# The first addition of a three-tap convolution, for batches 4, 5 and 6, by accumulating DMAs from SBUF to SBUF in place of VectorE

## The chip, the cores and the metric

The kernel runs on one core of a Trainium2 chip. The metric is the device time of one execution in microseconds (us), smaller is better; a kernel is run several times and the median is taken. Profiles are of one execution each; times in them count from the start of the profile's span.

## The reference

Two stages run in sequence: a linear attention with a normalisation, and a feed-forward block whose gate comes from a convolution along the sequence. Shapes: 8 batches, 8 heads of 64, sequence 576, model width 512, inner width 1024.

```python
kv  = einsum('bhsd,bhse->bhde', k, v)
o   = einsum('bhsd,bhde->bhse', q, kv)
x   = o / sqrt(mean(o*o, -1) + 1e-6) * g_norm        # heads side by side: (8, 576, 512)
h   = maximum(x @ w_in, 0)                           # (8, 576, 1024)
c   = conv_w[0]*h[s-1] + conv_w[1]*h[s] + conv_w[2]*h[s+1]   # per channel, zero outside the sequence
out = (h * sigmoid(c)) @ w_out                       # (8, 576, 512), float32
```

## The kernel before

Features lie on the 128 partitions and the sequence along the free dimension, in bf16. The inner width of 1024 makes eight feature tiles (index f), the model width four (index t). Two batches share one tile of x and one tile of h.

The order of all work is written out by hand in one string, ORDER. Its tokens are operations with their indices, such as `hm.6.0`; a loop calls them in turn, and a last loop fixes that each engine runs its instructions in exactly this order. Semaphores between the engines come from the tile framework. The operations that matter here, with the engine and the line in the profile of before:

- `Lq`, `Lk`, `Lv` (L148): loads of a batch of q, k, v from HBM, issued from GpSimd's queue, cast to bf16 on the way.
- `sp.b.t` (L411, TensorE) and `mu.b.t` (L417, VectorE): the normalising factor is spread over the partitions in PSUM, and x is made of it, one of four tiles t of batch b.
- `hm.b.f` (L434, TensorE): one feature tile of h from all four tiles of x; `re.b.f` (L440, ScalarE) takes it out of PSUM with a relu.
- the convolution of a chunk c, for a pair j of feature tiles (f = 2j and 2j+1): `ta.c.f` (L459, VectorE) makes the three products of a feature tile with its tap weights, in a buffer `tap` of three parts; there are two such buffers. `ad.c.j` adds the three parts for both tiles of the pair, in two instructions: the first part, shifted by one, is added to the middle one (L466), then the last part, shifted the other way (L467). `sg.c.j` (L473, ScalarE) takes the sigmoid in place, and `mg.c.j` (L479, VectorE) multiplies h by it.
- `om.p.m` (L524, TensorE): 128 rows of the output of batch pair p, from all eight tiles of h; `ea` (L530, ScalarE) copies them from PSUM and `st` (L540) stores them, from SP's queue.

Chunks of the convolution are, by the table CONV: batch 0 (on TensorE), 1, 2 and 3 together, 4 and 5 together (chunk 3), 6 (chunk 4), and 7 (chunk 5). Chunk 3's `tap` has two batches, chunk 4's has one. So an `ad` of chunk 3 adds 2 x 2 x 575 elements on each partition in each instruction, one of chunk 4 2 x 575.

PSUM has two pools: three buffers (`ps_a`) for h, x's factors and the transposes, two (`ps_b`) for the output rows. Since each engine's order is fixed, an instruction that waits holds up all that stand behind it on its engine.

Of the kernel before, what the change touches and what calls it, by code (L numbers as in the profile page):

```python
# [54 lines left out]
AL = mybir.AluOpType  # L55
# [4 lines left out]
BUFS = {'a': 3, 'b': 2, 'q': 2, 'k': 2, 'v': 2, 'qT': 5, 'sq': 8, 'o32': 8, 'xT': 2, 'h': 2, 'tap': 2, 'row': 8, 'w': 2, 'gate': 3}  # L60

ORDER = """
di.4 di.7 di.6 qt.0.0 qc.0.0 qt.0.1 kv.0.0.1 kvc.0.0.1.0 kvc.0.0.1.1 ot.0.0 di.5 kv.0.1.1 sq.0.0 qc.0.1 on.0
di.2 kvc.0.1.1.0 nl.0 kvc.0.1.1.1 ot.0.1 sq.0.1 kv.0.2.1 nx.0 on.1 kvc.0.2.1.1 mu0.0 kvc.0.2.1.0 di.1 Lk.1
Lv.1 nl.1 nx.1 kv.0.3.1 ot.0.2 kvc.0.3.1.1 sq.0.2 on.2 kvc.0.3.1.0 nl.2 mu0.1 ot.0.3 sq.0.3 on.3 ws.1 Lq.1
ws.2 nx.2 mu0.2 nl.3 ws.0 nx.3 mu0.3 hm.0.0 hm.0.7 re.0.7 re.0.0 kv.1.0.4 kvc.1.0.4.0 Lw hm.0.5 Lk.2 Lv.2 Lq.2
re.0.5 hm.0.2 re.0.2 qt.1.0 kvc.1.0.4.1 hm.0.4 re.0.4 qc.1.0 ot.1.0 qt.1.1 qc.1.1 ot.1.1 sq.1.0 oc.1.1 sq.1.1
ot.1.2 sq.1.2 di.0 ot.1.3 sq.1.3 oc.1.3 oc.1.2 ss.1 ln.0 hm.0.1 Lk.3 ex.0 re.0.1 Lv.3 hm.0.6 di.3 Lq.3 oc.1.0
hm.0.3 cv.0.0 re.0.6 sl.0 sp.1.0 mu.1.0 re.0.3 sv.0.0 cv.0.4 sp.1.1 kv.2.0.4 sv.0.4 Lk.4 sp.1.3 mu.1.1
kvc.2.0.4.1 mv.0.0 mu.1.3 sp.1.2 mu.1.2 cv.0.6 cv.0.2 sv.0.6 hm.1.0 mv.0.6 qt.2.1 sv.0.2 mv.0.4 mv.0.2 qc.2.1  # L70
kvc.2.0.4.0 hm.1.1 re.1.0 re.1.1 ot.2.3 ta.1.0 cv.0.7 sq.2.3 sv.0.7 hm.1.4 Lv.4 oc.2.3 cv.0.5 qt.2.0 ta.1.1
ad.1.0 re.1.4 sv.0.5 sg.1.0 hm.1.5 re.1.5 qc.2.0 ot.2.1 mg.1.0 cv.0.1 sq.2.1 sv.0.1 oc.2.1 ot.2.0 sq.2.0
oc.2.0 kv.3.0.4 kvc.3.0.4.0 ta.1.4 Lq.4 qt.3.0 qc.3.0 hm.1.6 hm.1.7 kvc.3.0.4.1 ta.1.5 mv.0.7 re.1.6 re.1.7
ot.3.0 oc.3.0 sq.3.0 mv.0.1 qt.3.1 cv.0.3 qc.3.1 ot.3.3 sv.0.3 oc.3.3 ta.1.6 Lk.5 Lv.5 ta.1.7 ot.3.2 sq.3.3
sq.3.2 ot.3.1 oc.3.2 mv.0.3 ot.2.2 kv.4.0.4 sq.3.1 sq.2.2 oc.3.1 hm.1.2 ss.2 re.1.2 ss.3 ad.1.3 ln.1 ex.1
kvc.4.0.4.0 Lq.5 qt.4.1 qt.4.0 ad.1.2 mv.0.5 qc.4.1 hm.1.3 qc.4.0 kvc.4.0.4.1 om.0.2 re.1.3 oc.2.2 sl.1 sp.2.0
mu.2.0 sg.1.3 sp.3.2 mu.3.2 sp.2.2 om.0.0 mu.2.2 mg.1.3 sp.2.3 ot.4.2 Lk.6 Lv.6 mu.2.3 ea.0.2 sp.2.1 om.0.3
mu.2.1 oc.4.2 ot.4.3 sq.4.2 ea.0.0 ta.1.2 sp.3.3 mu.3.3 sq.4.3 oc.4.3 sp.3.0 mu.3.0 ta.1.3 kv.5.0.4 sg.1.2
sp.3.1 kvc.5.0.4.0 hm.2.0 hm.2.5 ea.0.3 mu.3.1 ad.1.1 re.2.0 re.2.5 hm.2.4 qt.5.0 kvc.5.0.4.1 re.2.4 qc.5.0
sg.1.1 qt.5.1 qc.5.1 hm.2.2 re.2.2 ot.4.1 oc.4.1 sq.4.1 st.0.0 mg.1.2 hm.3.4 re.3.4 Lq.6 Lk.7 Lv.7 Lq.7 mg.1.1  # L80
hm.3.5 re.3.5 ot.5.3 oc.5.3 sq.5.3 hm.3.2 hm.3.3 re.3.2 ot.5.0 hm.2.3 ta.2.4 re.3.3 sq.5.0 ta.2.5 re.2.3
ot.5.2 sq.5.2 oc.5.0 oc.5.2 om.0.4 ot.4.0 ta.2.2 ot.5.1 hm.3.6 oc.4.0 ad.2.2 ta.2.3 sq.5.1 ea.0.4 sq.4.0
om.0.5 ss.4 ss.5 oc.5.1 re.3.6 qt.6.0 ea.0.5 ln.2 qt.7.0 qt.6.1 ex.2 ad.2.1 qc.6.0 om.0.8 ea.0.8 sg.2.1 qc.6.1
om.0.1 sl.2 sp.4.0 ea.0.1 sp.4.2 qc.7.0 sp.5.1 kv.6.0.4 mu.4.0 hm.3.0 mu.5.1 mu.4.2 mg.2.1 sp.5.0 hm.3.1
mu.5.0 re.3.0 re.3.1 sp.4.3 kv.7.0.4 kvc.7.0.4.0 kvc.6.0.4.0 sp.5.3 kvc.7.0.4.1 hm.2.1 re.2.1 mu.4.3 ta.2.0
hm.2.6 sp.4.1 st.0.8 mu.5.3 kvc.6.0.4.1 sg.2.2 sp.5.2 ta.2.1 mu.4.1 om.0.7 hm.3.7 re.2.6 ad.2.0 mg.2.2 re.3.7
sg.2.0 mu.5.2 om.0.6 hm.2.7 re.2.7 hm.4.0 ea.0.6 hm.5.1 ta.2.6 re.5.1 hm.4.3 re.4.3 ta.2.7 ea.0.7 hm.5.0
re.5.0 re.4.0 hm.5.5 re.5.5 hm.5.2 re.5.2 st.0.3 ad.2.3 mg.2.0 st.0.7 qt.7.1 hm.4.1 hm.5.4 sg.2.3 re.4.1
qc.7.1 re.5.4 hm.4.5 re.4.5 hm.4.2 ot.6.1 re.4.2 ta.3.0 oc.6.1 hm.5.3 sq.6.1 mg.2.3 ot.6.3 om.1.5 ot.6.0
re.5.3 ot.7.1 oc.6.3 sq.6.3 ea.1.5 ot.6.2 sq.6.0 oc.7.1 om.1.2 ta.3.1 ta.3.2 oc.6.0 ta.3.3 ad.3.0 ot.7.3  # L90
oc.6.2 sq.6.2 ea.1.2 st.0.6 om.1.6 ot.7.0 sq.7.1 hm.4.4 om.1.8 sg.3.0 re.4.4 ea.1.6 sq.7.0 sq.7.3 ot.7.2
st.1.2 ad.3.1 sq.7.2 ea.1.8 oc.7.3 om.1.3 ea.1.3 ss.6 ss.7 ln.3 hm.5.6 st.0.1 mg.3.0 ta.3.4 re.5.6 ta.3.5
ad.3.2 om.1.4 hm.4.7 st.0.5 ex.3 om.1.0 oc.7.2 sl.3 oc.7.0 st.1.5 sp.6.0 mu.6.0 sp.6.3 re.4.7 mu.6.3 sg.3.1
ea.1.4 hm.4.6 re.4.6 sp.7.0 mu.7.0 hm.5.7 re.5.7 sp.6.2 om.1.7 st.0.4 ea.1.0 mg.3.1 sp.7.3 ea.1.7 mu.6.2
sg.3.2 ta.3.6 sp.6.1 sp.7.2 mu.7.2 om.1.1 mu.6.1 hm.6.0 re.6.0 st.0.2 hm.6.2 re.6.2 ta.3.7 mg.3.2 ad.3.3
ea.1.1 st.1.1 hm.6.1 re.6.1 hm.6.3 re.6.3 hm.6.4 re.6.4 hm.6.5 sg.3.3 mu.7.3 ta.4.2 sp.7.1 hm.6.6 mu.7.1
ta.4.3 mg.3.3 hm.6.7 re.6.5 re.6.7 hm.7.6 hm.7.2 re.7.6 st.1.0 ad.4.1 re.6.6 re.7.2 hm.7.3 sg.4.1 hm.7.4
ta.4.4 hm.7.0 re.7.4 ta.4.5 mg.4.1 re.7.0 hm.7.7 hm.7.5 ad.4.2 st.1.8 ta.4.0 ta.4.1 re.7.7 hm.7.1 om.2.2
sg.4.2 mg.4.2 ea.2.2 st.1.7 om.2.8 ea.2.8 st.2.8 ta.4.6 ad.4.0 sg.4.0 ta.4.7 ad.4.3 om.2.0 re.7.5 ea.2.0
mg.4.0 om.2.7 ta.5.6 om.2.4 sg.4.3 mg.4.3 ta.5.7 ea.2.7 ea.2.4 ta.5.4 om.2.3 re.7.3 st.2.0 ea.2.3 ad.5.3  # L100
sg.5.3 re.7.1 ta.5.5 om.2.1 ea.2.1 ad.5.2 mg.5.3 st.1.6 st.1.4 om.2.6 ta.5.2 sg.5.2 mg.5.2 st.2.1 ea.2.6
st.2.7 ta.5.0 st.2.4 ta.5.3 ta.5.1 om.2.5 ea.2.5 om.3.0 om.3.1 ad.5.1 ad.5.0 ea.3.0 st.3.0 ea.3.1 st.3.1
sg.5.1 om.3.2 mg.5.1 om.3.3 sg.5.0 ea.3.2 ea.3.3 st.1.3 mg.5.0 st.2.5 om.3.8 ea.3.8 st.3.3 st.2.3 st.2.6
om.3.5 ea.3.5 st.3.5 st.2.2 st.3.8 om.3.6 st.3.2 ea.3.6 st.3.6 om.3.4 ea.3.4 st.3.4 om.3.7 ea.3.7 st.3.7
"""


# [1 line left out]
def kernel(  # L109
# [11 lines left out]
    nc = tc.nc  # L121
    B, H, S, D = q.shape
# [33 lines left out]
    def load_w_in(eng, i):  # L156
# [9 lines left out]
        out=ident, in_=ident, compare_op=AL.not_equal, fill=1.0,  # L166
# [71 lines left out]
    T = {}  # L238
# [222 lines left out]
                h_tile(p)[:, f, bs, :].rearrange("p b s -> p (b s)"), cw[:, col:col + 1])  # L461

    @op
    def ad(c, j):
        tap = T["tap", c, j].rearrange("p m f b s -> p m (f b) s")
        nc.vector.tensor_add(tap[:, 1, :, 1:], tap[:, 1, :, 1:], tap[:, 0, :, :S - 1])  # L466
        nc.vector.tensor_add(tap[:, 1, :, :S - 1], tap[:, 1, :, :S - 1], tap[:, 2, :, 1:])  # L467

    @op
# [116 lines left out]
```

## Time and profile before

| | us |
|---|---|
| median of 3 runs | 204.3 (202.88 to 204.7) |
| span of the profiled execution, first to last instruction | 201.4 |
| TensorE busy | 175.6 (87%) |
| VectorE busy | 155.5 (77%) |
| ScalarE busy | 149.9 (74%) |
| GpSimd busy | 25.3 (13%) |
| L466, first additions, 20 instructions | 19.8 |
| L467, second additions, 20 instructions | 20.1 |

The profile comes with no time of its own for the profiled execution beside its span; the median of the runs is 2.9 us above that span. The granted clock of TensorE is full throughout. GpSimd's last load is issued at 81.7 us. The work of chunks 3 and 4 on VectorE lies between 120 and 174 us, that of chunk 5 from 172 to 189 us; the last 40 matmuls of the output follow.

### The profile page before, as it was taken

The page shows a single profiled execution, that of the slowest core. Times are in us where ns is not written, and L with a number is a line of the kernel's source. Part 1 is how long each engine was busy: PE and PEld are TensorE (multiplying, and loading weights), DVE is VectorE, ACT ScalarE, POOL GpSimd, SP SyncE. Part 2 cuts the span into 40 slices and gives each one's busy share as a digit, 9 for nine tenths or more (in the row PEclk, how much of TensorE's full clock was granted, in tenths as well). Part 3 has the DMA queues.
Part 4 walks back from the last instruction along what each step waited for, and adds up shares of the span by engine and source line. Part 5 has one row for each costly group of instructions (what it writes and reads, how often), then busy time and mean ns, then how long its engine had stood idle before and what let it go on. Part 6 is the DMA issues. An engine that isn't in the chain of part 4 may idle for free.

```text
span 201.4 us, 4356 instructions
## 1 busy us (share of the span) xinstructions
PE 175.6 (87%) x1783; PEld 111.7 (55%) x1801; DVE 155.5 (77%) x325; ACT 149.9 (74%) x230; POOL 25.3 (13%) x38
## 2 busy tenths in 40 slices
PE   0057389799998999999999999999999999999792
PEld 0044057477775557766576776445667774444340
DVE  3096931368879799799899999989799999999400
ACT  2008816995999989999778899999978865684532
POOL 7383303103132303100000000000000000000000
PEclk9999999999999999999999999999999999999999
DMA  5999999999999999970200020080005001423654
GB/s 129 143 215 315 201 204 205 204 203 204 203 192 203 201 204 173 200 119 5 104 3 3 0 104 3 0 312 2 3 0 208 0 3 48 161 107 116 248 229 188
DMA packets 26295, 27.03 MB, mean 134 GB/s; under 512 B 1292, under 2 KB 21284, under 8 KB 26276
## 3 DMA queue, kind: packets, MB, share of 16 engines
q0 software_dynamic: 20368, 16.78, 52.1%
q1 hardware_dynamic: 5908, 9.98, 13.1%
q8 instruction: 14, 0.23, 0.5%
q14 instruction: 5, 0.04, 0.1%
HBM read 32.52 MB, written 9.44 MB: 208 GB/s over the span
## 4 chain that ended last, share of the span: by engine, by line
PE 60%; DVE 26%; ACT 6%; DMA 3%; issue 2%; SPq 1%; DVEq 0%; ACTq 0%
PE h_ps L434 25%; PE om_ps L524 18%; DVE tap L459 8%; DVE h L479 4%; PE qt_ps L296 4%; DMA cw_rows<-in_moe_conv_w_dram 3%; DVE tap L467 3%; PE kv_ps L272 3%; PE sp_ps L411 3%; DVE tap L466 3%; PE cv_ps L500 3%; PE o_ps L309 2%; DVE xT L417 2%; ACT tap L473 2%; DVE dg L488 2%
## 5 line engine op out<-in xcount | busy, mean ns | idle before, releaser
L434 PE MATMUL h_ps<-xT,w_in_sb 128*128 128x288 bf16 x512 | 69.9, 291 | 2.9 <-DVE w_in_sb L261 2.2
L524 PE MATMUL om_ps<-w_out_sb,h 128*128 128x512 bf16 x278 | 64.1, 379 | 1.5 <-DVE h L479 1.0
L434 PEld LDWEIGHTS <-w_in_sb 128*128 128x128 bf16 x512 | 49.9, 99 | 18.6 <-DVE w_in_sb L261 2.3
L440 ACT ACTIVATE h<-h_ps 128x576 bf16<-128x576 f32 x64 | 41.0, 656 | 13.5 <-PE h_ps L434 13.2
L524 PEld LDWEIGHTS <-h 128*128 128x128 bf16 x288 | 28.0, 98 | 32.3 <-DVE h L479 1.5
L459 DVE TENSOR_SCALAR tap<-h,cw 128x576 bf16<-128x576 bf16 (+1 forms) x120 | 43.8, 429 | 1.7 <-ACT h L440 1.3
L530 ACT ACTIVATE row<-om_ps 128x512 f32<-128x512 f32 x36 | 22.1, 616 | 15.1 <-PE om_ps L524 14.5
L473 ACT ACTIVATE tap<-tap 128x1152 bf16<-128x1152 bf16 (+1 forms) x20 | 31.1, 1553 | 1.7 <-DVE tap L467 1.5
L417 DVE TENSOR_TENSOR xT<-o,sp_ps 128x576 bf16<-128x576 f32 x28 | 20.1, 749 | 4.0 <-PE sp_ps L411 3.7
L479 DVE TENSOR_TENSOR h<-h,tap 128x1152 bf16<-128x1152 bf16 (+1 forms) x20 | 19.8, 994 | 1.8 <-ACT tap L473 1.8
L467 DVE TENSOR_TENSOR tap<-tap 128x1150 bf16<-128x1150 bf16 (+1 forms) x20 | 20.1, 1004 | 0.7
L303 DVE COPY qT<-qt_ps 128x1152 bf16<-128x1152 bf16 x16 | 11.8, 754 | 11.0 <-PE qt_ps L296 10.9
L466 DVE TENSOR_TENSOR tap<-tap 128x1150 bf16<-128x1150 bf16 (+1 forms) x20 | 19.8, 992 | 0.0
L328 ACT ACTIVATE sq<-o_ps 128x576 bf16<-128x576 f32 x28 | 18.2, 687 | 0.5 <-PE o_ps L309 0.5
L334 ACT ACTIVATE o<-o_ps 128x576 f32<-128x576 f32 x28 | 18.1, 675 | 0.2 <-PE o_ps L309 0.2
L286 ACT ACTIVATE kvbd<-kv_ps 64x256 bf16<-64x256 f32 (+1 forms) x18 | 6.0, 339 | 11.8 <-PE kv_ps L272 11.6
L148 POOL DMA_DIRECT2D k_sb<-in_k_dram x11 | 8.0, 728 | 36.9 <-PE kv_ps L272 36.9
L296 PE MATMUL qt_ps<-ident,q_sb 96*64 96x96 bf16 x384 | 11.2, 217 | 1.2 <-DMA q_sb<-in_q_dram 0.9
L296 PEld LDWEIGHTS <-q_sb 96*64 96x64 bf16 x384 | 9.7, 117 | 3.1 <-issue 2.1
L411 PE MATMUL sp_ps<-wparts,spread 128*128 128x288 bf16 x56 | 9.8, 286 | 0.2 <-DVE xT L417 0.2
L308 PE MATMUL o_ps<-qT,kvbd 128*128 128x64 bf16 x32 | 6.3, 196 | 4.0 <-DVE kvbd L284 1.7
L272 PEld LDWEIGHTS <-k_sb 96*64 96x64 bf16 x384 | 7.9, 122 | 3.3 <-issue 3.3
(57 smaller groups left out, 122.5 us busy)
## 6 DMA issues: line engine op xcount, KB each, us to landing
out_dram<-row SPq DMA_DIRECT2D x36, 256.0 KB, 2.3
q_sb<-in_q_dram POOLq DMA_DIRECT2D x8, 576.0 KB, 11.4
k_sb<-in_k_dram POOLq DMA_DIRECT2D x7, 576.0 KB, 10.6
v_sb<-in_v_dram POOLq DMA_DIRECT2D x7, 576.0 KB, 12.5
w_stage<-in_moe_w_in_dram POOLq DMA_DIRECT2D x1, 1024.0 KB, 9.6
w_out_sb<-in_moe_w_out_dram POOLq DMA_DIRECT2D x1, 1024.0 KB, 20.0
k_sb<-in_k_dram POOLq DMA_DIRECT2D x4, 144.0 KB, 9.1
v_sb<-in_v_dram POOLq DMA_DIRECT2D x4, 144.0 KB, 9.0
```

Of the source, the lines that this page charges most:

```text
L296: nc.tensor.transpose(ps[i * D:(i + 1) * D, tt, r * PS:(r + 1) * PS], q_sb[:, 2 * (2 * u + tt) + i, r * D:(r + 1) * D], ident[:PS, :PS])
L328: nc.scalar.activation(s.rearrange("p (n r) -> p n r", r=R), natural(src), AX.Square)
L417: nc.vector.tensor_mul(x_tile(b)[:, t, :].rearrange("p (e n) -> p e n", e=2), T["o32", b, t].rearrange("p (e n) -> p e n", e=2), T["sp", b ...
L434: nc.tensor.matmul(ps[:, e, :HS], w_in_sb[:, t, f * P:(f + 1) * P], x[:, t, e * HS:(e + 1) * HS], start=(t == 0), stop=(t == NT - 1))
L440: nc.scalar.activation(h_tile(b // 2)[:, f, b % 2, :].rearrange("p (e n) -> p e n", e=2), T["hm", b, f][:, :, :HS], AX.Relu)
L459: nc.vector.tensor_scalar_mul(tap[:, m, f % 2, :, :].rearrange("p b s -> p (b s)"), h_tile(p)[:, f, bs, :].rearrange("p b s -> p (b s)"), ...
L466: nc.vector.tensor_add(tap[:, 1, :, 1:], tap[:, 1, :, 1:], tap[:, 0, :, :S - 1])
L467: nc.vector.tensor_add(tap[:, 1, :, :S - 1], tap[:, 1, :, :S - 1], tap[:, 2, :, 1:])
L473: nc.scalar.activation(tap, tap, AX.Sigmoid)
L479: nc.vector.tensor_mul(h, h, T["tap", c, j][:, 1])
L524: nc.tensor.matmul(ps, h[:, f, m * P:(m + 1) * P], w_out_sb[:, f, :], start=(f == 0), stop=(f == NF - 1))
L530: nc.scalar.activation(T["os", p, m], T["om", p, m], AX.Copy)
```

## The change

For chunks 3 and 4 the first addition leaves VectorE. A new operation `aa.c.j` issues two DMAs from GpSimd's queue, one for each feature tile of the pair; each reads the first part of `tap` and adds it to the middle part in SBUF. The second addition stays on VectorE, as the only instruction of these chunks' `ad`. In ORDER each `aa.c.j` stands right behind the second `ta` of its pair, and two of the `ad` stand later than before:

- `ad.3.2` stood behind `ta.3.5`; it now stands behind `mu.6.3`.
- `ad.3.0` still follows `ta.3.3`, `ad.3.3` still follows `mg.3.2`, `ad.4.1` follows `mg.3.3`, `ad.4.2` follows `mg.4.1`.
- `ad.3.1` still follows `ad.3.0`, `ad.4.0` still follows `ta.4.6`.
- `ad.4.3` stood behind `ta.4.7`; it now stands behind `mg.4.0`.

On VectorE two positions thus differ (`ad.3.2` and `ad.4.3`), beside the eight instructions that are gone; the orders of TensorE, ScalarE and SP are the same.

```diff
     @op
+    def aa(c, j):
+        for f in range(2):
+            tap = T["tap", c, j][:, :, f]
+            nc.gpsimd.dma_start(out=tap[:, 1, :, 1:], in_=tap[:, 0, :, :S - 1], accum_op=AL.add)
+
+    @op
     def ad(c, j):
         tap = T["tap", c, j].rearrange("p m f b s -> p m (f b) s")
-        nc.vector.tensor_add(tap[:, 1, :, 1:], tap[:, 1, :, 1:], tap[:, 0, :, :S - 1])
+        if c not in (3, 4):
+            nc.vector.tensor_add(tap[:, 1, :, 1:], tap[:, 1, :, 1:], tap[:, 0, :, :S - 1])
         nc.vector.tensor_add(tap[:, 1, :, :S - 1], tap[:, 1, :, :S - 1], tap[:, 2, :, 1:])
```

The part of ORDER that changes, before and after, cut to VectorE's and GpSimd's tokens:

```
before: ... ta.3.1 ta.3.2 ta.3.3 ad.3.0 ad.3.1 mg.3.0 ta.3.4 ta.3.5 ad.3.2 sl.3 mu.6.0 mu.6.3 mu.7.0 mg.3.1
        mu.6.2 ta.3.6 mu.7.2 mu.6.1 ta.3.7 mg.3.2 ad.3.3 mu.7.3 ta.4.2 mu.7.1 ta.4.3 mg.3.3 ad.4.1 ta.4.4 ta.4.5
        mg.4.1 ad.4.2 ta.4.0 ta.4.1 mg.4.2 ta.4.6 ad.4.0 ta.4.7 ad.4.3 mg.4.0 ta.5.6 mg.4.3 ...
after:  ... ta.3.1 aa.3.0 ta.3.2 ta.3.3 aa.3.1 ad.3.0 ad.3.1 mg.3.0 ta.3.4 ta.3.5 aa.3.2 sl.3 mu.6.0 mu.6.3 ad.3.2 mu.7.0 mg.3.1
        mu.6.2 ta.3.6 mu.7.2 mu.6.1 ta.3.7 aa.3.3 mg.3.2 ad.3.3 mu.7.3 ta.4.2 mu.7.1 ta.4.3 aa.4.1 mg.3.3 ad.4.1 ta.4.4 ta.4.5
        aa.4.2 mg.4.1 ad.4.2 ta.4.0 ta.4.1 aa.4.0 mg.4.2 ta.4.6 ad.4.0 ta.4.7 aa.4.3 mg.4.0 ad.4.3 ta.5.6 mg.4.3 ...
```

More of the change, by code (lines that the diff above doesn't have):

```diff
@@ L62 @@
 ORDER = """
[L63 to L102, printed above, removed]
@@ L103 @@
-sg.5.1 om.3.2 mg.5.1 om.3.3 sg.5.0 ea.3.2 ea.3.3 st.1.3 mg.5.0 st.2.5 om.3.8 ea.3.8 st.3.3 st.2.3 st.2.6
-om.3.5 ea.3.5 st.3.5 st.2.2 st.3.8 om.3.6 st.3.2 ea.3.6 st.3.6 om.3.4 ea.3.4 st.3.4 om.3.7 ea.3.7 st.3.7
+di.4 di.7 di.6 qt.0.0 qc.0.0 qt.0.1 kv.0.0.1 kvc.0.0.1.0 kvc.0.0.1.1 ot.0.0 di.5 kv.0.1.1 sq.0.0 qc.0.1 on.0 di.2
+kvc.0.1.1.0 nl.0 kvc.0.1.1.1 ot.0.1 sq.0.1 kv.0.2.1 nx.0 on.1 kvc.0.2.1.1 mu0.0 kvc.0.2.1.0 di.1 Lk.1 Lv.1 nl.1 nx.1
+kv.0.3.1 ot.0.2 kvc.0.3.1.1 sq.0.2 on.2 kvc.0.3.1.0 nl.2 mu0.1 ot.0.3 sq.0.3 on.3 ws.1 Lq.1 ws.2 nx.2 mu0.2 nl.3 ws.0
@@ new lines @@
+nx.3 mu0.3 hm.0.0 hm.0.7 re.0.7 re.0.0 kv.1.0.4 kvc.1.0.4.0 Lw hm.0.5 Lk.2 Lv.2 Lq.2 re.0.5 hm.0.2 re.0.2 qt.1.0
+kvc.1.0.4.1 hm.0.4 re.0.4 qc.1.0 ot.1.0 qt.1.1 qc.1.1 ot.1.1 sq.1.0 oc.1.1 sq.1.1 ot.1.2 sq.1.2 di.0 ot.1.3 sq.1.3
+oc.1.3 oc.1.2 ss.1 ln.0 hm.0.1 Lk.3 ex.0 re.0.1 Lv.3 hm.0.6 di.3 Lq.3 oc.1.0 hm.0.3 cv.0.0 re.0.6 sl.0 sp.1.0 mu.1.0
+re.0.3 sv.0.0 cv.0.4 sp.1.1 kv.2.0.4 sv.0.4 Lk.4 sp.1.3 mu.1.1 kvc.2.0.4.1 mv.0.0 mu.1.3 sp.1.2 mu.1.2 cv.0.6 cv.0.2
+sv.0.6 hm.1.0 mv.0.6 qt.2.1 sv.0.2 mv.0.4 mv.0.2 qc.2.1 kvc.2.0.4.0 hm.1.1 re.1.0 re.1.1 ot.2.3 ta.1.0 cv.0.7 sq.2.3
@@ new lines @@
+sv.0.7 hm.1.4 Lv.4 oc.2.3 cv.0.5 qt.2.0 ta.1.1 ad.1.0 re.1.4 sv.0.5 sg.1.0 hm.1.5 re.1.5 qc.2.0 ot.2.1 mg.1.0 cv.0.1
+sq.2.1 sv.0.1 oc.2.1 ot.2.0 sq.2.0 oc.2.0 kv.3.0.4 kvc.3.0.4.0 ta.1.4 Lq.4 qt.3.0 qc.3.0 hm.1.6 hm.1.7 kvc.3.0.4.1
+ta.1.5 mv.0.7 re.1.6 re.1.7 ot.3.0 oc.3.0 sq.3.0 mv.0.1 qt.3.1 cv.0.3 qc.3.1 ot.3.3 sv.0.3 oc.3.3 ta.1.6 Lk.5 Lv.5
+ta.1.7 ot.3.2 sq.3.3 sq.3.2 ot.3.1 oc.3.2 mv.0.3 ot.2.2 kv.4.0.4 sq.3.1 sq.2.2 oc.3.1 hm.1.2 ss.2 re.1.2 ss.3 ad.1.3
+ln.1 ex.1 kvc.4.0.4.0 Lq.5 qt.4.1 qt.4.0 ad.1.2 mv.0.5 qc.4.1 hm.1.3 qc.4.0 kvc.4.0.4.1 om.0.2 re.1.3 oc.2.2 sl.1
@@ new lines @@
+sp.2.0 mu.2.0 sg.1.3 sp.3.2 mu.3.2 sp.2.2 om.0.0 mu.2.2 mg.1.3 sp.2.3 ot.4.2 Lk.6 Lv.6 mu.2.3 ea.0.2 sp.2.1 om.0.3
+mu.2.1 oc.4.2 ot.4.3 sq.4.2 ea.0.0 ta.1.2 sp.3.3 mu.3.3 sq.4.3 oc.4.3 sp.3.0 mu.3.0 ta.1.3 kv.5.0.4 sg.1.2 sp.3.1
+kvc.5.0.4.0 hm.2.0 hm.2.5 ea.0.3 mu.3.1 ad.1.1 re.2.0 re.2.5 hm.2.4 qt.5.0 kvc.5.0.4.1 re.2.4 qc.5.0 sg.1.1 qt.5.1
+qc.5.1 hm.2.2 re.2.2 ot.4.1 oc.4.1 sq.4.1 st.0.0 mg.1.2 hm.3.4 re.3.4 Lq.6 Lk.7 Lv.7 Lq.7 mg.1.1 hm.3.5 re.3.5 ot.5.3
+oc.5.3 sq.5.3 hm.3.2 hm.3.3 re.3.2 ot.5.0 hm.2.3 ta.2.4 re.3.3 sq.5.0 ta.2.5 re.2.3 ot.5.2 sq.5.2 oc.5.0 oc.5.2 om.0.4
@@ new lines @@
+ot.4.0 ta.2.2 ot.5.1 hm.3.6 oc.4.0 ad.2.2 ta.2.3 sq.5.1 ea.0.4 sq.4.0 om.0.5 ss.4 ss.5 oc.5.1 re.3.6 qt.6.0 ea.0.5
+ln.2 qt.7.0 qt.6.1 ex.2 ad.2.1 qc.6.0 om.0.8 ea.0.8 sg.2.1 qc.6.1 om.0.1 sl.2 sp.4.0 ea.0.1 sp.4.2 qc.7.0 sp.5.1
+kv.6.0.4 mu.4.0 hm.3.0 mu.5.1 mu.4.2 mg.2.1 sp.5.0 hm.3.1 mu.5.0 re.3.0 re.3.1 sp.4.3 kv.7.0.4 kvc.7.0.4.0 kvc.6.0.4.0
+sp.5.3 kvc.7.0.4.1 hm.2.1 re.2.1 mu.4.3 ta.2.0 hm.2.6 sp.4.1 st.0.8 mu.5.3 kvc.6.0.4.1 sg.2.2 sp.5.2 ta.2.1 mu.4.1
+om.0.7 hm.3.7 re.2.6 ad.2.0 mg.2.2 re.3.7 sg.2.0 mu.5.2 om.0.6 hm.2.7 re.2.7 hm.4.0 ea.0.6 hm.5.1 ta.2.6 re.5.1 hm.4.3
@@ new lines @@
+re.4.3 ta.2.7 ea.0.7 hm.5.0 re.5.0 re.4.0 hm.5.5 re.5.5 hm.5.2 re.5.2 st.0.3 ad.2.3 mg.2.0 st.0.7 qt.7.1 hm.4.1 hm.5.4
+sg.2.3 re.4.1 qc.7.1 re.5.4 hm.4.5 re.4.5 hm.4.2 ot.6.1 re.4.2 ta.3.0 oc.6.1 hm.5.3 sq.6.1 mg.2.3 ot.6.3 om.1.5 ot.6.0
+re.5.3 ot.7.1 oc.6.3 sq.6.3 ea.1.5 ot.6.2 sq.6.0 oc.7.1 om.1.2 ta.3.1 aa.3.0 ta.3.2 oc.6.0 ta.3.3 aa.3.1 ad.3.0 ot.7.3
+oc.6.2 sq.6.2 ea.1.2 st.0.6 om.1.6 ot.7.0 sq.7.1 hm.4.4 om.1.8 sg.3.0 re.4.4 ea.1.6 sq.7.0 sq.7.3 ot.7.2 st.1.2 ad.3.1
+sq.7.2 ea.1.8 oc.7.3 om.1.3 ea.1.3 ss.6 ss.7 ln.3 hm.5.6 st.0.1 mg.3.0 ta.3.4 re.5.6 ta.3.5 aa.3.2 om.1.4 hm.4.7
@@ new lines @@
+st.0.5 ex.3 om.1.0 oc.7.2 sl.3 oc.7.0 st.1.5 sp.6.0 mu.6.0 sp.6.3 re.4.7 mu.6.3 ad.3.2 sg.3.1 ea.1.4 hm.4.6 re.4.6
+sp.7.0 mu.7.0 hm.5.7 re.5.7 sp.6.2 om.1.7 st.0.4 ea.1.0 mg.3.1 sp.7.3 ea.1.7 mu.6.2 sg.3.2 ta.3.6 sp.6.1 sp.7.2 mu.7.2
+om.1.1 mu.6.1 hm.6.0 re.6.0 st.0.2 hm.6.2 re.6.2 ta.3.7 aa.3.3 mg.3.2 ad.3.3 ea.1.1 st.1.1 hm.6.1 re.6.1 hm.6.3 re.6.3
+hm.6.4 re.6.4 hm.6.5 sg.3.3 mu.7.3 ta.4.2 sp.7.1 hm.6.6 mu.7.1 ta.4.3 aa.4.1 mg.3.3 hm.6.7 re.6.5 re.6.7 hm.7.6 hm.7.2
+re.7.6 st.1.0 ad.4.1 re.6.6 re.7.2 hm.7.3 sg.4.1 hm.7.4 ta.4.4 hm.7.0 re.7.4 ta.4.5 aa.4.2 mg.4.1 re.7.0 hm.7.7 hm.7.5
@@ new lines @@
+ad.4.2 st.1.8 ta.4.0 ta.4.1 aa.4.0 re.7.7 hm.7.1 om.2.2 sg.4.2 mg.4.2 ea.2.2 st.1.7 om.2.8 ea.2.8 st.2.8 ta.4.6 ad.4.0
+sg.4.0 ta.4.7 aa.4.3 om.2.0 re.7.5 ea.2.0 mg.4.0 ad.4.3 om.2.7 ta.5.6 om.2.4 sg.4.3 mg.4.3 ta.5.7 ea.2.7 ea.2.4 ta.5.4
+om.2.3 re.7.3 st.2.0 ea.2.3 ad.5.3 sg.5.3 re.7.1 ta.5.5 om.2.1 ea.2.1 ad.5.2 mg.5.3 st.1.6 st.1.4 om.2.6 ta.5.2 sg.5.2
+mg.5.2 st.2.1 ea.2.6 st.2.7 ta.5.0 st.2.4 ta.5.3 ta.5.1 om.2.5 ea.2.5 om.3.0 om.3.1 ad.5.1 ad.5.0 ea.3.0 st.3.0 ea.3.1
+st.3.1 sg.5.1 om.3.2 mg.5.1 om.3.3 sg.5.0 ea.3.2 ea.3.3 st.1.3 mg.5.0 st.2.5 om.3.8 ea.3.8 st.3.3 st.2.3 st.2.6 om.3.5
@@ L105 @@
+ea.3.5 st.3.5 st.2.2 st.3.8 om.3.6 st.3.2 ea.3.6 st.3.6 om.3.4 ea.3.4 st.3.4 om.3.7 ea.3.7 st.3.7
 """
```

## The prediction

> **What bounds the kernel now.** I read the page first (span, busy shares), then the timelines of TensorE and of VectorE from 120 us on, because all that the change touches runs there, and last the rows that can price a DMA. Between this execution's span, 201.4 us, and the median of the runs, 204.3 us, lie 2.9 us that the trace doesn't show; I add my sum to the span and then these 2.9 us.
>
> ```profile
> span 201.4 us, 4356 instructions
> ...
> PE 175.6 (87%) x1783; PEld 111.7 (55%) x1801; DVE 155.5 (77%) x325; ACT 149.9 (74%) x230; POOL 25.3 (13%) x38
> ```
>
> The second view is TensorE's timeline (start, busy us, line).
>
> ```profile
> 149.29 6.04 PE L434 MATMUL h_ps<-xT,w_in_sb 128*128 128x288 bf16 x48
> ...
> 155.42 10.24 PE L434 MATMUL h_ps<-xT,w_in_sb 128*128 128x288 bf16 x80
> 165.71 22.39 PE L524 MATMUL om_ps<-w_out_sb,h 128*128 128x512 bf16 x101
> 189.09 8.81 PE L524 MATMUL om_ps<-w_out_sb,h 128*128 128x512 bf16 x40 [0.98 <-DVE h L479]
> ```
>
> TensorE runs without a gap from 136 to 188 us and idles 0.98 us before the last 40 matmuls, for VectorE's last product (mg.5.0, done 189.03). With one gap of 0.22 us at 135.8 that is all the idle time that this view marks after 120 us (1.6 us by its busy time, slivers included). So relieving VectorE can bring 0.98 us here at most: TensorE then has no wait on it left. But the reverse doesn't hold, as the third view, VectorE's timeline, shows.
>
> ```profile
> 149.16 1.37 DVE L459 TENSOR_SCALAR tap<-h,cw 128x1152 bf16<-128x1152 bf16 x3
> 150.45 1.35 DVE L479 TENSOR_TENSOR h<-h,tap 128x2304 bf16<-128x2304 bf16 x1
> 151.72 1.35 DVE L466 TENSOR_TENSOR tap<-tap 128x2300 bf16<-128x2300 bf16 x1
> 153.10 1.36 DVE L467 TENSOR_TENSOR tap<-tap 128x2300 bf16<-128x2300 bf16 x1
> 154.38 0.74 DVE L417 TENSOR_TENSOR xT<-o,sp_ps 128x576 bf16<-128x576 f32 x1
> 155.04 0.93 DVE L459 TENSOR_SCALAR tap<-h,cw 128x576 bf16<-128x576 bf16 x3
> 155.88 0.75 DVE L417 TENSOR_TENSOR xT<-o,sp_ps 128x576 bf16<-128x576 f32 x1
> 156.54 0.93 DVE L459 TENSOR_SCALAR tap<-h,cw 128x576 bf16<-128x576 bf16 x3
> 157.38 1.35 DVE L479 TENSOR_TENSOR h<-h,tap 128x2304 bf16<-128x2304 bf16 x1
> 158.65 0.76 DVE L466 TENSOR_TENSOR tap<-tap 128x1150 bf16<-128x1150 bf16 x1
> 159.44 0.76 DVE L467 TENSOR_TENSOR tap<-tap 128x1150 bf16<-128x1150 bf16 x1
> ...
> 188.27 0.76 DVE L479 TENSOR_TENSOR h<-h,tap 128x1152 bf16<-128x1152 bf16 x1 [0.63 <-ACT tap L473]
> ```
>
> These are, in order: ta.3.7, mg.3.2, the two additions of ad.3.3, mu.7.3, ta.4.2, mu.7.1, ta.4.3, mg.3.3, the two additions of ad.4.1. VectorE is also full, and some of its results have no slack: mu.7.1 ends at 156.63 and the first matmuls of batch 7 come some 0.8 us later. VectorE's order is in one line, so a wait inside it delays everything behind it.
>
> **The change part by part.** Removed: 8 first additions (L466), 4 of 128x2300 (1.35 us, a step of 1.38 to the next start) and 4 of 128x1150 (0.75, step 0.79): 8.7 us of VectorE's time. Three of the large ones lie before 139.5 us, where VectorE next waits for ScalarE's Exp (L391, ends 139.5) and then for sp_ps until 142.38; what is saved there goes into these waits.
>
> Added: 16 DMAs on GpSimd's queue, two for each aa; two of 128x2x575 elements (294 KB each) for chunk 3, of 128x575 (147 KB) for chunk 4. That queue is empty after its last load at 81.7 us, so nothing is behind them; SP's stores are untouched and share the DMA engines, which are 13% busy from 157 to 174 us and 37% from 174 to 189. The price is a wait: each ad of chunks 3 and 4 now waits for the landing of a DMA that can be issued only after the second ta of its pair. Call the time from the end of that ta to the landing L2 (chunk 3) and L1 (chunk 4).
>
> No row shows an accumulating transfer, or one from SBUF to SBUF. The nearest:
>
> ```profile
> q1 hardware_dynamic: 5908, 9.98, 13.1%
> ...
> out_dram<-row SPq DMA_DIRECT2D x36, 256.0 KB, 2.3
> ```
>
> ```profile
> 2.51 0.64 POOL L148 DMA_DIRECT2D k_sb<-in_k_dram  x1
> ```
>
> ```profile
> DMA to landing us min/median/max: 5.7/9.9/23.1
> ```
>
> A store from SBUF (128 rows, 8 for each engine) lands in 2.3 us. Its queue's 5908 packets took 13.1% of 16 x 201.4 us, 71 ns each, so 8 rows are 0.57 us and 1.73 us is fixed. GpSimd's issue of a load of 192 rows took 0.64 us. An accumulation must read two operands, so I double the rows: L1 = 0.64 + 1.73 + 2 x 0.57 = 3.5 us; with 16 rows for each engine L2 = 0.64 + 1.73 + 4 x 0.57 = 4.65 us. The lower bound is the fastest store, 2.0 us, for all; the upper the fastest of GpSimd's loads, 5.7 us for 768 rows, for all. I take the middle values since the store is the nearest row: SBUF side, one row for each partition.
>
> Now VectorE's line with these waits. ad.3.0 and ad.3.1 wait (landing 123.9 + 4.65 and 126.7 + 4.65 = 131.3), but mg.3.0 and ta.3.4, ta.3.5 still end near 137, ahead of the Exp at 139.5: cost nothing up to L2 = 7.6 us. The changed order puts ad.3.2 behind mu.6.3, past the idle time that covered it; its landing (137 + 4.65) is over by then, but its second addition, 1.3 us, now stands between mu.6.3 and mu.7.0, so mu.7.0, mg.3.1, mu.6.2 and mu.6.1 are 1.3 us late, and TensorE's hm.6.0, which follows mu.6.1 by 0.05 us, with them. ta.3.7 then ends at 151.75 instead of 150.45; the landing is at 156.4, with only mg.3.2 (1.27) in between; ad.3.3 ends at 157.7, and mu.7.3, ta.4.2, mu.7.1 behind it at 159.8 instead of 156.54: 3.3 us late (L2 - 1.35). Behind the same wait on ScalarE stand sg.3.3 and re.6.5, and on TensorE all of batch 7.
>
> Chunk 4, from the end of mu.7.1 to the end of mg.4.3, took 156.54 to 173.59 = 17.05 us. Now each pair of ta is followed by a landing that has only one or two short instructions to cover it (mg.3.3 1.27; mg.4.1 0.67; mg.4.2 and ta.4.6 1.63; a wait for the sigmoid and mg.4.0, 1.16): all inside L1. So: ta.4.3 0.84, L1, ad 0.76, two ta 1.67, L1, ad 0.76, two ta 1.67, L1, ad 0.76, ta.4.7 0.84, L1, ad 0.76, ta.5.6 0.93, the sigmoid's rest 0.32, mg.4.3 0.75: 10.06 + 4 L1 = 24.06, 7.0 us more. What follows, chunk 5 (173.59 to 189.03), is unchanged and still a line without slack, and the last 40 matmuls follow it. TensorE, 3.3 us late from batch 7 on, would have its 13 chunks of L524 (1.73 us each, from 169.0) done by 191.5, 8 us before mg.5.0 at 199.3. ScalarE's copies out of om_ps stand behind sigmoids that wait for the same landings, and can take most of these 8 us; VectorE still sets the end.
>
> Sum: L2 + 4 L1 - 8.34 = 4.65 + 14.0 - 8.34 = +10.3 us; span 211.7, time 214.6 us. With the bounds 2.0 and 5.7 for both it is +1.7 and +20.2 us: 206.0 and 224.5.
>
> Two rules of the Trainium skill bear on this. The page "DMA: Bandwidth & Descriptors", section "Anatomy of one DMA — SWDGE (gpsimd) path", fits a DMA of GpSimd's to 2.0 us plus its bytes at 436 GB/s; by that L1 = 2.34 and L2 = 2.68, and the time would be 208.0 us, an estimate; no run here shows it for an accumulation. The page "SBUF — State Buffer", section "Who interferes with whom", says that VectorE's two-port instructions, tensor_scalar among them, lock GpSimd out while it writes descriptors. It speaks against the change, since each first DMA of a pair is issued just as the next ta starts. The trace shows a milder thing: where a load's issue (0.77 us) falls on three tensor_scalars, they take 1.21 us instead of 0.92.
>
> ```profile
> 77.15 1.21 DVE L459 TENSOR_SCALAR tap<-h,cw 128x576 bf16<-128x576 bf16 x3
> ```
>
> **The rivals.** *Not slower: the landing is hidden.* If L2 + 4 L1 stay under 8.34 us, 1.67 us each, no stall outlasts what is saved; TensorE's 0.98 us wait goes and nothing else can: 203.3 us, no measurable change. For it: the DMA engines are nearly free then. Against it: not one of the 36 stores landed under 2.0 us, and GpSimd's issue comes on top.
>
> *The accumulation runs at the pace of the loads,* or slower: 5.7 us for each landing, 224.5 us. For it: the loads are GpSimd's only transfers here. Against it: they read HBM with full engines and have three to six times the rows.
>
> *GpSimd and VectorE hold each other up.* On the late line two first DMAs (aa.4.2, aa.4.0) fall on the next ta, 0.29 us each, and five last DMAs may take 0.12 longer to issue (the longest load issue was 0.89): +1.2 us, 215.8 us. Against it: VectorE mostly stands idle or multiplies tensors when the deciding DMA is issued.
>
> That the change doesn't do what it says I exclude: the built order shows the 8 additions gone and the 16 DMAs in place, TensorE's, ScalarE's and SP's orders being the same.
>
> **How the numbers follow.** Forecast 0.68, loads' pace 0.15, mutual hindrance 0.11, hidden 0.06. A measurement here can tell about 1%, 2.0 us, from no change. Faster by that needs more than all of TensorE's idle time after 120 us (1.6 us): 0.01. Within it: 0.05, the hidden landing. Slower: 0.94. The range goes from 207.5 (landings of 2.3 us each) to 224.0, just short of the loads' pace; a bit under 2 in 10 lies outside.
>
> **What would show it.** L466's count falls from 20 to 12, 16 DMA issues appear on GpSimd; their landing, median 2.5 to 4.5 us, decides most. VectorE's idle time before L467's successor (line 471), released by DMAs, should be some 12 to 13 us on the late line (3.4 before the last addition of chunk 3; 2.2, 2.8, 1.9 and 2.3 in chunk 4) and a few hidden us before 137; TensorE should wait 3 us or more in h_ps of batch 7, and the rest of the loss among and before the last om_ps. Wrong I am if that line shows no idle time, if the landing is under 1.7 us or over 6, or if the end is set by something other than VectorE's line.

## The result, and the profile after

The changed kernel takes 210.7 us (median of 4 runs, 210.2 to 211.4), the kernel before 203.6 us (202.5 to 204.7). The ratio is 1.035, 95% interval 1.031 to 1.039: 7.1 us slower.

From the page of the changed kernel: the span, the busy shares, and the groups of the added and the halved work. The columns of a group are busy time, mean ns of one, idle time of the engine before it and what ended most of that; the last two lines are DMA issues with their size and the time to landing.

```profile
span 209.6 us, 4398 instructions
...
PE 178.2 (85%) x1783; PEld 112.3 (54%) x1801; DVE 148.2 (71%) x317; ACT 149.6 (71%) x230; POOL 41.9 (20%) x54
...
L464 POOL DMA_DIRECT2D tap<-tap x16 | 16.7, 1079 | 77.5 <-DVE tap L456 64.5
L471 DVE TENSOR_TENSOR tap<-tap 128x1150 bf16<-128x1150 bf16 (+1 forms) x20 | 20.1, 1004 | 13.8 <-DMA tap<-tap 13.4
...
L470 DVE TENSOR_TENSOR tap<-tap 128x1150 bf16<-128x1150 bf16 (+1 forms) x12 | 11.4, 950 | 0.0
...
tap<-tap POOLq DMA_DIRECT2D x8, 287.5 KB, 4.6
tap<-tap POOLq DMA_DIRECT2D x8, 143.8 KB, 2.8
```

VectorE lost its 8 additions (its busy time falls by 7.3 us), and got 13.4 us of waiting in front of the second additions (L471), ended by the DMAs. Its timeline over the place that the prediction worked through:

```profile
150.49 1.37 DVE L456 TENSOR_SCALAR tap<-h,cw 128x1152 bf16<-128x1152 bf16 x3
151.77 1.35 DVE L483 TENSOR_TENSOR h<-h,tap 128x2304 bf16<-128x2304 bf16 x1
155.64 1.36 DVE L471 TENSOR_TENSOR tap<-tap 128x2300 bf16<-128x2300 bf16 x1 [2.52 <-DMA tap<-tap]
156.92 0.74 DVE L414 TENSOR_TENSOR xT<-o,sp_ps 128x576 bf16<-128x576 f32 x1
...
160.00 1.35 DVE L483 TENSOR_TENSOR h<-h,tap 128x2304 bf16<-128x2304 bf16 x1
162.90 0.77 DVE L471 TENSOR_TENSOR tap<-tap 128x1150 bf16<-128x1150 bf16 x1 [1.55 <-DMA tap<-tap]
163.57 1.76 DVE L456 TENSOR_SCALAR tap<-h,cw 128x576 bf16<-128x576 bf16 x6
165.25 0.75 DVE L483 TENSOR_TENSOR h<-h,tap 128x1152 bf16<-128x1152 bf16 x1
168.51 0.76 DVE L471 TENSOR_TENSOR tap<-tap 128x1150 bf16<-128x1150 bf16 x1 [2.51 <-DMA tap<-tap]
...
174.13 0.76 DVE L471 TENSOR_TENSOR tap<-tap 128x1150 bf16<-128x1150 bf16 x1 [1.56 <-DMA tap<-tap]
...
178.88 0.76 DVE L471 TENSOR_TENSOR tap<-tap 128x1150 bf16<-128x1150 bf16 x1 [1.94 <-DMA tap<-tap]
...
196.40 0.76 DVE L483 TENSOR_TENSOR h<-h,tap 128x1152 bf16<-128x1152 bf16 x1 [0.29 <-ACT tap L477]
```

There is one wait in chunk 3 (ad.3.3) and four in chunk 4 (ad.4.1, 4.2, 4.0, 4.3), each with only one or two short instructions between the end of a ta and the landing. L2, from the start of mg.3.2 (the end of ta.3.7) to ad.3.3, is 155.64 - 151.77 = 3.87 us; L1 is 2.90, 3.26, 3.27 and 3.23 us, in sum 12.66. The last product, mg.5.0, starts at 196.40 instead of 188.27: 8.1 us late, and the span is 8.2 us longer. Of this, 0.3 us is a difference between the two executions from before the first DMA (118.38 instead of 118.09 us for the same multiplication).

### The profile page after: what moved, and what is told of

Same layout as the page of the kernel before. It is cut to its first block, busy times and chain, and to the rows that moved or that the text cites. A ratio compares the mean times of both kernels' runs of the same rounds, so it can differ in the third digit from the quotient of the medians.

```text
span 209.6 us, 4398 instructions
## 1 busy us (share of the span) xinstructions
PE 178.2 (85%) x1783; PEld 112.3 (54%) x1801; DVE 148.2 (71%) x317; ACT 149.6 (71%) x230; POOL 41.9 (20%) x54
## 5 line engine op out<-in xcount | busy, mean ns | idle before, releaser
L528 PE MATMUL om_ps<-w_out_sb,h 128*128 128x512 bf16 x278 | 66.1, 386 | 4.7 <-ACT row L534 4.0
L456 DVE TENSOR_SCALAR tap<-h,cw 128x576 bf16<-128x576 bf16 (+1 forms) x120 | 44.1, 430 | 1.6 <-ACT h L437 1.3
L464 POOL DMA_DIRECT2D tap<-tap x16 | 16.7, 1079 | 77.5 <-DVE tap L456 64.5
L471 DVE TENSOR_TENSOR tap<-tap 128x1150 bf16<-128x1150 bf16 (+1 forms) x20 | 20.1, 1004 | 13.8 <-DMA tap<-tap 13.4
L408 PE MATMUL sp_ps<-wparts,spread 128*128 128x288 bf16 x56 | 9.8, 286 | 2.1 <-DVE xT L414 1.5
L470 DVE TENSOR_TENSOR tap<-tap 128x1150 bf16<-128x1150 bf16 (+1 forms) x12 | 11.4, 950 | 0.0
## 6 DMA issues: line engine op xcount, KB each, us to landing
k_sb<-in_k_dram POOLq DMA_DIRECT2D x7, 576.0 KB, 10.1
```

The source lines that it names most:

```text
L456: nc.vector.tensor_scalar_mul(tap[:, m, f % 2, :, :].rearrange("p b s -> p (b s)"), h_tile(p)[:, f, bs, :].rearrange("p b s -> p (b s)"), ...
L528: nc.tensor.matmul(ps, h[:, f, m * P:(m + 1) * P], w_out_sb[:, f, :], start=(f == 0), stop=(f == NF - 1))
```

## The experiments

**Theory A**, the prediction's: the loss is VectorE's line, waiting for landings that nothing covers, plus what the moved ad add between the mu. **Rival B**: GpSimd's descriptor writing and the transfers slow VectorE itself. **Rival C**: the moved ad are what costs. **Rival D**, for what could be won at best: VectorE, not TensorE, is the bound.

### The parts one by one

`order_only`: the changed order, all additions on VectorE.

```diff
     def aa(c, j):
+        return
         for f in range(2):
...
-        if c not in (3, 4):
+        if True:
```

> The changed order, but no DMA: all additions of chunks 3 and 4 are on VectorE, where the changed order has their ad. Theory A (the loss is VectorE waiting for landings, plus the 1.3 us of ad.3.2 moved between the mu): ad.3.2 now stands there with both additions, 2.66 us, so mu.7.1 is 2.7 us late and the sigmoid's wait of mg.4.0 adds 0.4: some 3 us over before, about 206.7 us, and no idle time before the additions. Rival C (the moved ad are what costs): most of the 7.1 us measured for the whole change is here too, 209 to 211 us. Rival B (GpSimd's descriptor writing and the transfers slow VectorE down): nothing but the order's small price, 204 to 205.

Measured: 208.0 us against 203.9, ratio 1.021 (1.015 to 1.026): +4.1 us.

`only3`: DMAs for chunk 3 alone (`aa` returns for c == 4; `if c != 3` before the first addition).

> Chunk 3's first additions by DMA, chunk 4's back on VectorE, the changed order. A: one landing in the open, ad.3.3: 3.85 us from the end of ta.3.7 to the addition in the changed profile, so 3.85 - 1.35 = 2.5, and 0.5 for mg.4.0's wait: +3.0 us, about 206.6 us. B (cost by number and bytes of the DMAs; chunk 3 has two thirds of the bytes): +4.7 us, 208.3. C: as order_only.

Measured: 207.5 us, ratio 1.016 (1.011 to 1.021): +3.6 us.

`only4`: DMAs for chunk 4 alone, edited likewise.

> Chunk 4's first additions by DMA, chunk 3's back on VectorE, the changed order. A: the four landings of chunk 4, 3.17 us each in the changed profile, cost 4 x 3.17 - 7.05 = 5.6, and ad.3.2 stands with both additions between the mu, 2.66: +8.3 us, about 211.9 us, slower than the whole change although half the DMAs are gone. B (a third of the bytes): +2.4 us and the order's price, 206 to 207. C: as order_only.

Measured: 211.6 us, ratio 1.037 (1.033 to 1.041): +7.7 us.

A's three figures were +3.0, +3.0 and +8.3. Rival B falls as the cause of the loss: chunk 3 has two thirds of the bytes and half of the DMAs, and is no slower with them than without (207.5 against 208.0), while chunk 4's small ones cost 3.6 us over the order alone. C holds for a part, more than A gave it: the order alone costs 4.1 us, 1.0 more than A's sum. The reason is in two lines of `order_only`'s VectorE timeline, of mu.7.1 and of mg.4.0:

```profile
158.52 0.75 DVE L414 TENSOR_TENSOR xT<-o,sp_ps 128x576 bf16<-128x576 f32 x1
...
173.47 0.76 DVE L484 TENSOR_TENSOR h<-h,tap 128x1152 bf16<-128x1152 bf16 x1 [1.23 <-ACT tap L478]
```

mu.7.1 starts 2.64 us late (155.88 before), as the two additions of ad.3.2 between the mu say (2.66). But mg.4.0 then waits 1.23 us for its sigmoid and not 0.4: on ScalarE that sigmoid, at 172.29 us, stands behind a copy of output rows for which ScalarE waits 1.13 us, until TensorE has made the rows (171.79). The tile's additions had ended at 171.40. In chunk 3 the landing in the open and the additions saved are worth the same: mu.7.1 starts at 158.42 in the changed kernel.

### What could be won at best

`left_out`: the order of before, the 8 first additions done by nobody (`if c not in (3, 4)` before L466).

> The order of before, with the 8 first additions of chunks 3 and 4 left out altogether: neither VectorE nor a DMA does them, so the convolution of batches 4 to 6 misses its first tap. This is what the change could bring at best. A (TensorE is the bound, with one wait of 0.98 us on VectorE): -1.0 us, about 202.6 us, although 8.7 us of VectorE's work are gone; TensorE runs without a gap to the end. Rival D (VectorE's line is the bound): -4.5 us, the five steps after 143 us, or more.

Measured: 204.1 us against 203.9, ratio 1.002 (0.998 to 1.005): no difference. Rival D falls, and A's -1.0 us with it. TensorE's timeline shows the wait still there, and the waits show why (engine, line, what it waited for; us in total, times, longest):

```profile
190.71 8.81 PE L525 MATMUL om_ps<-w_out_sb,h 128*128 128x512 bf16 x40 [0.96 <-DVE h L480]
```

```profile
DVE h L480 <- ACT tap L474: 7.3, 6, 3.4
```

The time that VectorE saved became waits for sigmoids, 7.3 us from 100 us on (3.4 of them before mg.3.0, 3.2 in chunk 4). The sigmoids stand on ScalarE in a fixed order, in chunk 4 among copies out of om_ps: the one that mg.4.0 waits for starts at 171.28 us, behind a copy for which ScalarE waits 1.13 us on TensorE, although its additions had ended at 169.50. So VectorE can't run ahead of TensorE here, and arrives at chunk 5, which is unchanged, no earlier than before: behind mg.4.3 it goes on at 175.22 instead of 173.59 us, in an execution whose TensorE is 1.65 us behind that of before already at batch 7 (157.07 and 155.42).

### What a landing is made of

`plain`: the same DMAs without `accum_op`, overwriting the middle part.

> The changed kernel with plain copies of the same bytes in place of the accumulating DMAs, so that the middle part is overwritten and not added to: it prices the accumulation itself. Theory A1 (the time from the end of a ta to the landing is GpSimd's issue and a fixed latency; reading a second operand costs nothing that counts): issue 0.86 and 1.2 us, landing 2.8 us after the issue starts for 147 KB as with the accumulation, about 210.7 us. Theory A2 (an accumulation reads twice and takes twice the engines' time, as the prediction doubled it): 0.57 us less for each landing of chunk 4 and 1.1 less for that of chunk 3: about 207.3 us.

`plain_sp`: the same copies by `nc.sync.dma_start`.

> The same plain copies, issued from SP's queue, among the stores of the output rows; again overwritten, not added to. Theory A3 (GpSimd's issue, 0.86 to 1.2 us, and the second issue waiting for the first, 0.3 us, are a third of each landing): a store's issue is 0.43 us, so each landing comes 0.4 to 0.8 us earlier than in the run with GpSimd's plain copies, 2 to 4 us of time. If the latency lies behind the issue: the same time as with GpSimd's plain copies, or worse by stores held up behind copies that wait.

Measured: 207.1 us, ratio 1.015 (1.008 to 1.022), and 206.4 us, ratio 1.012 (1.005 to 1.019). The pages of the two, first GpSimd's copies, then SP's:

```profile
L464 POOL DMA_DIRECT2D tap<-tap x16 | 11.4, 711 | 78.3 <-ACT h L437 39.1
...
tap<-tap POOLq DMA_DIRECT2D x8, 287.5 KB, 2.6
tap<-tap POOLq DMA_DIRECT2D x8, 143.8 KB, 2.0
```

```profile
tap<-tap SPq DMA_DIRECT2D x8, 287.5 KB, 2.6
tap<-tap SPq DMA_DIRECT2D x8, 143.8 KB, 2.0
```

A1 falls, and the size is near A2's: counted from the start of the issue, 147 KB land in 2.0 us as a copy and 2.8 as an accumulation. (That the second operand takes the time is not shown by this.) Part of the 0.8 us is GpSimd's issue, from these timelines of GpSimd, first the changed kernel's for tiles 4.1 and 4.2, then `plain`'s for 4.1:

```profile
158.77 0.90 POOL L464 DMA_DIRECT2D tap<-tap  x1 [5.85 <-DVE tap L456]
160.10 0.86 POOL L464 DMA_DIRECT2D tap<-tap  x1 [0.43 <-DVE tap L456]
164.75 1.74 POOL L464 DMA_DIRECT2D tap<-tap  x2 [3.79 <-DVE tap L456]
```

```profile
160.08 0.55 POOL L464 DMA_DIRECT2D tap<-tap  x1 [0.67 <-DVE tap L456]
```

The accumulation takes 0.86 us to issue, the copy 0.55; so 0.3 of the 0.8 us is issue and 0.5 lies behind it. The x2 shows why L1 is 2.90 for tile 4.1 and 3.26 for 4.2: two ta of 0.84 us each follow each other, the first issue takes 0.87, and the second DMA starts late. Tile 4.3's L1 of 3.23 us comes of a start some 0.4 us after its last ta (176.04), which the x2 doesn't explain. A3 falls: SP's copies land no sooner than GpSimd's, and the two times, of two runs each, can't be told apart with these intervals. Neither time is a clean price of the landings, since the order alone already takes 208.0 us.

### The landings covered

`cover4`: the order of before; accumulating DMAs for tiles 4.2, 4.0 and 4.3 alone, each second addition moved behind other work. `cover4_vec`: the same order and buffers, all additions on VectorE.

```diff
             if c == 4:
+                two = work.tile([P, 2, 3, 2, n, S], BF16, name="tap", tag="tap", bufs=BUFS["tap"])
+                for s, jj in enumerate((1, 2) if j in (1, 2) else (0, 3)):
+                    T["tap", c, jj] = two[:, s]
...
-        nc.vector.tensor_add(tap[:, 1, :, 1:], tap[:, 1, :, 1:], tap[:, 0, :, :S - 1])
+        if (c, j) not in ((4, 2), (4, 0), (4, 3)):
+            nc.vector.tensor_add(tap[:, 1, :, 1:], tap[:, 1, :, 1:], tap[:, 0, :, :S - 1])
```

```
VectorE, GpSimd: ... ta.4.4 ta.4.5 aa.4.2 mg.4.1 ta.4.0 ta.4.1 aa.4.0 ta.4.6 ad.4.2 ta.4.7 aa.4.3 mg.4.2 ad.4.0 ta.5.6 ta.5.7
                 mg.4.0 ad.4.3 ad.5.3 mg.4.3 ta.5.4 ta.5.5 ad.5.2 mg.5.3 ta.5.2 ta.5.3 mg.5.2 ...
ScalarE: sg.4.0 ahead of ea.2.8, sg.5.1 ahead of ea.3.1
```

> The order of before up to mg.4.1, chunk 3 on VectorE; accumulating DMAs for the first additions of tiles 4.2, 4.0 and 4.3 alone, with each of their second additions moved behind 2.5 to 4 us of other work: the next ta, the multiplication of the tile before, and the first ta of chunk 5. For this two taps of chunk 4 share one buffer of chunk 3's size. Three sigmoids are moved ahead of copies of output rows on ScalarE. Theory A (only landings in the open cost): nearly no idle time before these additions, VectorE 1 to 2 us ahead in chunk 5, TensorE's wait of 1 us before the last 40 matmuls gone: -0.6 to -1.0 us, about 203.1 us. Rival E (the run with the additions left out shows that VectorE is held by sigmoids that queue behind the output copies on ScalarE): the wait stays, 203.9 us. Rival B (the DMAs slow the other engines): over before.

> The order and buffers of the run with covered landings, without DMAs: all additions on VectorE. It tells the order's share of that run from the DMAs'. Theory A: three additions of 0.78 us more on VectorE's line, 2.3 us, against the 1 to 2 us that it was ahead: TensorE's wait is back, 203.9 to 205 us, 1 to 2 us over the run with DMAs. If the gain there comes from the order alone: the same time as that run.

Measured: `cover4` 202.6 us against 204.0, ratio 0.993 (0.991 to 0.996), 1.4 us faster than the kernel before; `cover4_vec` 203.9 us, ratio 0.999 (0.996 to 1.002), no difference. TensorE's timelines, of `cover4` and then of `cover4_vec`:

```profile
165.76 31.03 PE L533 MATMUL om_ps<-w_out_sb,h 128*128 128x512 bf16 x141
```

```profile
165.83 5.13 PE L533 MATMUL om_ps<-w_out_sb,h 128*128 128x512 bf16 x23
171.89 26.35 PE L533 MATMUL om_ps<-w_out_sb,h 128*128 128x512 bf16 x118 [0.93 <-ACT row L539]
```

And one of the covered additions, ad.4.2, in `cover4`'s VectorE timeline:

```profile
162.50 2.60 DVE L461 TENSOR_SCALAR tap<-h,cw 128x576 bf16<-128x576 bf16 x9
165.23 0.76 DVE L476 TENSOR_TENSOR tap<-tap 128x1150 bf16<-128x1150 bf16 x1
```

No second addition of chunk 4 waits for a DMA by this trace, although these DMAs land no sooner (3.2 us in the median). TensorE runs without a gap from 165.8 us to its end. Rival E's tie, shown for the order of before, may be loosened by the moved sigmoids (two change their place on ScalarE, not three as the expectation says). Without the DMAs the same order leaves TensorE a gap of 0.93 us, so the gain needs the DMAs. Whether it needs the moved sigmoids was not tried apart. This is the fastest kernel here, and still a small gain: TensorE has no more to give back in this stretch.

## Why the prediction was right

**The mechanism and the place** were right: five waits, on VectorE's line, each ended by a DMA. Predicted were 3.4, 2.2, 2.8, 1.9 and 2.3 us, measured 2.52, 1.55, 2.51, 1.56 and 1.94. That is 10.1 us against some 12 to 13. The early tiles 3.0 and 3.1 wait 1.73 and 1.61 us at no cost, as predicted. The sum L2 + 4 L1 - 8.34 gives 3.87 + 12.66 - 8.34 = +8.2 us with the measured landings, and the spans of the two profiled executions differ by 8.2 us, or 7.9 without the 0.3 us from before the first DMA.

**The terms that were mis-sized** make 214.6 out of 210.7 us. L2 was put at 4.65 us and is 3.87, L1 at 3.5 and is 3.17 in the mean: together 0.8 + 4 x 0.33 = 2.1 us too much. The step that failed is adding GpSimd's issue (0.64) to a store's 2.3 us: the time to landing is counted from the start of the issue, so one issue was in it already. (The second DMA of tile 4.1 is issued at 160.10 us; with the 2.8 us of its group that makes 162.90, where ad.4.1 starts.) The doubling of the rows was about right (0.57 predicted, 0.5 us behind the issue measured). Another 0.9 us is the base: 2.9 us were taken to lie around the span of before, but for the changed kernel's runs span and time differ by 1.8 us (211.37 and 209.6), and for later runs of the kernel before by 2.0 to 2.1 us (204.48 and 202.5); the profiled execution of before thus took about 203.4 us, and a later run with the same span of 201.4 us took 203.42. 203.4 + 8.2 = 211.6 us is close to the 211.37 us of the profiled execution after, which was the slowest of its four runs; that is most of the rest.

**TensorE's share**: the prediction said that ScalarE's row copies, behind sigmoids that wait for the same landings, would take most of the 8 us that TensorE is ahead, and that VectorE would still set the end. The copies took 4.0 us by the profile's group of om_ps, in two waits of 1.71 and 2.32 us. Some 2 us more went to matmuls at half clock (that group is busy 66.1 us, 64.1 before), which the prediction doesn't have. In the 3.6 us before its last 40 matmuls TensorE is idle for only 0.2, so it was no longer ahead. Two lines of the changed kernel's ScalarE timeline show the tie:

```profile
193.66 0.60 ACT L534 ACTIVATE row<-om_ps 128x512 f32<-128x512 f32 x1 [1.08 <-PE om_ps L528]
194.16 2.21 ACT L477 ACTIVATE tap<-tap 128x1152 bf16<-128x1152 bf16 x2
```

The first of these two sigmoids stands behind the copy, and the second, for mg.5.0, behind the first, at 195.21 us; its additions end at 195.09. In the profile of before the same step takes 0.08 us (186.99 to 187.07), so VectorE's line explains the end to within 0.05 us, and TensorE's, held up by the same landings, comes out at the same time. That TensorE came out no later, half clock included, was luck. One sign failed: 3 us or more of waiting in h_ps of batch 7. TensorE waited 1.30 us before the factor's matmuls (L408) and 0.24 in h_ps, as it came there 1.1 us late already (150.36 instead of 149.29) and L2 was smaller.

**The rivals**: the loads' pace is out (landings of 2.8 and 4.6 us in the median; one DMA of tile 3.0 took 6.1, where the wait cost nothing). One reason against it was misread: the load that landed in 5.7 us is one of 144 KB, which is 192 rows and not 768. That lies between the 128 and the 256 rows of the accumulations, and is not three to six times as many. Mutual hindrance is there and small on VectorE: nine tensor_scalars beside the first issues take 4.29 us instead of 4.14, and all 120 take 44.1 instead of 43.8. For the hidden landing the price was wrong: 203.3 us was the sum with TensorE's wait gone, but `left_out` shows that relief on VectorE alone brings nothing that can be measured (at most 0.4 us by its interval).

**The two rules**: the Trainium skill, "DMA: Bandwidth & Descriptors", section "Anatomy of one DMA — SWDGE (gpsimd) path", gives by its fit, as an estimate, 2.34 us for 147 KB and 2.68 for 294 KB. The plain copies measured 2.0 and 2.6 here, the accumulations 2.8 and, for ad.3.3's, 3.8 from issue to landing: for the accumulation the measurement decides. The page "SBUF — State Buffer", section "Who interferes with whom", would have GpSimd locked out during tensor_scalar. In the changed kernel three issues that fall on tensor_scalars (from 124.11 us on) take 1.19 to 1.21 us each, and one beside other work (149.34) takes 1.19. In `cover4`, where most issues fall on tensor_scalars, the six take 0.90 to 1.55 us, 1.12 in the median, against 0.86 for the same shape in the changed kernel. So the lock-out is not seen as a rule, and GpSimd may be held up at times; these runs don't tell when.

## What to carry to other kernels

A DMA that takes an addition from a busy engine replaces work by latency: here 0.75 to 1.35 us of addition against 2.9 to 3.9 us from the last operand to the landing. Of the kernels here it paid only in the one whose consumers were moved that far back in their engine's order. Ask first who is the bound in that stretch, and which fixed orders (here sigmoids behind row copies) tie the relieved engine to it. Read whether a time to landing already contains the issue before adding one.

## What the runs showed that was not expected

TensorE's granted clock fell to half after a stretch with little work. The windows of the changed kernel (us, then each engine's busy time, then the clock):

```profile
176.00:180.00 4.00, 1.89 (x8) 0.78 (x8) 1.88 (x4) 1.44 (x4) 0.86 (x1) 1.00 0.69 212
180.00:182.00 2.00, 0.58 (x2) 0.25 (x2) 1.56 (x5) 2.00 (x4) 0.00 (x0) 0.88 0.12 47
182.00:184.00 2.00, 2.00 (x6) 0.74 (x5) 2.00 (x6) 0.40 (x1) 0.00 (x0) 0.50 0.00 0
```

From 176 to 182 us it was busy for 2.5 of 6 us; the matmuls that followed then ran at 0.50 clock. `only4` shows the same at the same place, `order_only`, with waits under 0.6 us there, does not. Finer windows of the changed kernel put the half clock between 181.53 and 184.94 us, 3.4 us long. It cost the end next to nothing here, since VectorE's line came out at the same time, but a wait on TensorE can cost more than its own length. The Trainium skill, "TensorE: Matmul & The Clock Gate", section "What's actually happening", has the clock halved after an idle window of some 3.4 us. No wait here was that long: they were 1.71 and 2.32 us with eight matmuls between them, and the clock fell all the same. What share of idle time is enough, no run here shows.

An accumulating DMA takes GpSimd 0.86 us to issue for 128 rows and about 1.2 us for 256, longer than the copy of the same shape (0.55 and 0.71): two in a row hold each other up.
